# A recurrence and attention kernel on one core: the 16x16 inverse blocks are turned by VectorE on chip, K's products go to GpSimd, and the block products are spread over the steps

## The chip, the core and the metric

One core of a Trainium2 chip runs the whole program once. The metric is the device time of one execution in microseconds (us); lower is better. The engines are named as in the profile: PE is TensorE's matmuls, PEld its weight loads, DVE is VectorE, ACT is ScalarE, POOL is GpSimd, SP is the queue of SyncE that issues nearly all DMAs.

## What is computed

A recurrence over 768 tokens for 32 heads with a 40x40 state, then a causal attention with four experts, of which two are mixed for each token. The change touches the recurrence alone:

```python
for t in range(S):
    y[:, :, t] = np.einsum('bhd,bhde->bhe', rt, state)
    Sa = np.einsum('bhde,bhe->bhd', state, at)
    state_decay = state * wt[:, :, None, :] - np.einsum('bhd,bhe->bhde', Sa, bt)
    state = state_decay + np.einsum('bhd,bhe->bhde', vt, kt)
```

Then `_moe_ref` takes y as x: q, k, v of each expert, causal softmax, `a @ v @ wo`, mixed by the gate of the two chosen experts.

## The kernel before

**Stages.** The recurrence is done in chunks of 32 tokens. Six windows of four chunks make the 768 tokens, and in a window each chunk is done in four units of eight heads, so that there are 96 units, 16 to a window. Attention follows, from about 480 us on; it is not touched.

**A round.** The main loop of `recurrence` runs n = 0 to 99. In each round it issues one stage of several units, in the order of `MAIN`: u, g, y, f, t, k, v (the slots 0 to 6). Nothing is scheduled by the compiler here: every engine takes its instructions in the order in which the loop writes them. Extra work is hung on a round and a slot by tables of strings: `SIDE` and `SIDE2` (preparing the next window), `EARLY` (window 0) and `INV` (the inverse). In a string the parts between slashes are the slots, a digit is the group of heads, a letter is the step. n0 is 16(W-1) for window W; the numbers in the tables are rounds after n0, and window 1's `INV` is three rounds later.

**Preparing a window** (`prep`), for each of four groups i: a and s are scans over the decays (lines 247, 253); b and c fetch and invert four elements; x and y multiply a by the decays (line 256); k and l on VectorE (line 261), or p on GpSimd (line 258), multiply K and b by the decays into the tile KB, which m, n, N and M use as weights of the matmuls at line 274. VectorE moves their result with a mask into GL (line 277). o stores 32x32 blocks to a buffer in DRAM, Ld. w, v and e load the inputs of the next group (EW, EA and EK of one buffer each, so that each load waits for the last reader of its buffer). `START` does window 0 and 1 with p on GpSimd; windows 2 to 5 use k and l.

**The inverse** (`invert`). Each 32x32 block, one a partition, 128 at a time in the tile MT, is unit triangular. L loads MT from Ld; C sets the diagonal to one and zeroes the block M12; T runs the 28 instructions that invert both 16x16 diagonal blocks (line 305), by VectorE in window 0, by GpSimd in windows 1 to 5. Then MT must be turned, so that the block's columns lie on partitions (tile TT), and the first diagonal block must be there in a second form for the block products. In window 0 VectorE does this by five 32x32 transposes (lines 313 and 315, the second form into rows 32 to 63 of GL). In windows 1 to 5 it goes through DRAM: S stores MT to Td; X copies the 16x16 block on GpSimd (line 309) and stores it to Tx; eight rounds after L, I loads Tx into GL (line 320) and B loads TT from Td by four DMAs with rows of 32 elements (line 318).

**The block products** fill the off-diagonal 16x16 block of the inverse, for a chunk c of a window: F(c) is 32 matmuls of 16x32 by 16x16 (line 325) and an ACT copy into N (line 327), H(c) is 32 matmuls with N (line 333) and an ACT copy into TT (line 334). u and g of the chunk's units read TT and GL.

**SP** issues in order, and a DMA that waits for a buffer holds all behind it. The loads of a chunk (RB, VT, VG, RT) go out one chunk ahead.

Of the kernel before, what the change touches and what calls it, by code (L numbers as in the profile page):

```python
# [7 lines left out]
F32 = mybir.dt.float32  # L8
AF = mybir.ActivationFunctionType
# [8 lines left out]
NW, NG, C = 6, 4, 32  # L18
# [1 line left out]

START = """Z0 E4 0apbc E5 0sx 1a 1b 0y 1c 0d 1sx 2a 0n E7 0q E6 1py 0m 2b 0o 1d 2pcs 1n R1 1q 2x 3a 2Yq 1m 3b 2m 3p
2d 3csx 1o 3y 2n 4a 3m 2o 4pb 3n 4c 5a 3d 4sy 3o 5b L 3q R0 4x R2 V00 V10 5cs V11 5xp 6a C 5y V01 Z1 4q 6b
T28 B F0 4m H0 6cspx 4dno 6Y 7a E8 7b 5d 7c 5q 7spYx k0"""
EARLY = {
    0: "/7d/F1/7q 5n/5m 5o",
    1: "6n/H1/6m/6o",
# [20 lines left out]
    -5: "///3y 2N 3k 3l///3ve",
    -4: "///0M 3m 0dqo",
    -3: "///1M 3N 1dqo",
    -2: "///2Mdqo",  # L50
# [2 lines left out]

SIDE2 = {
    -15: "///0abcs///0w",
    -14: "/0kly//0X///0ev",
    -13: "///1abc",
    -12: "///1s 0m 1x///1w",
    -11: "///1y 1k 1l///1ve",
    -10: "///2a 1m 2bc",  # L60
    -9: "///2s 2x///2w",
    -8: "///2y 0N 2k 2l///2ve",
    -7: "///3a 2m 3bc",
    -6: "///3s 1N 3x///3w",
    -5: "///3y 2N 3k 3l///3ve",
    -4: "///0M 3m 0dqo",
    -3: "///1M 3N 1dqo",
    -2: "///2Mdqo",
    -1: "///3Mdqo",
}  # L70
INV = {0: "L", 1: "C T4", 2: "T6", 3: "T6", 4: "T6", 5: "T6", 6: "S X", 8: "I B", 12: "//F0", 13: "//F1 H0", 14: "//F2 H1", 15: "//F3 H2", 16: "//H3"}
YE = "AA"


# [32 lines left out]

def constants():
    f = np.float32
    cm = np.zeros((128, 211), f)  # L110
    cm[:, :128] = np.eye(128)
    j = np.arange(32)
    m = (j[:, None] < j[None, :]).astype(f)
    cm[:32, 128:160] = m
    cm[32:64, 128:160] = m
    cm[:32, 160:192] = m
    cm[32:64, 160:192] = -m
    cm[64:128, 128:192] = cm[0:64, 128:192]
    p = np.arange(128)
    cm[:, 195:211] = (p[:, None] % 32 - 16 == np.arange(16)[None, :])  # L120
    return {"CM": cm}


def recurrence(tc, ctx, I, xT, CM, early, tail=None):
    nc = tc.nc
    ep = early.enter_context(tc.tile_pool(name="early", bufs=1, side="right"))
    sp = ctx.enter_context(tc.tile_pool(name="rec", bufs=1))
    dp = ctx.enter_context(tc.tile_pool(name="scr", bufs=1, space=DRAM))
    pp = ctx.enter_context(tc.tile_pool(name="rps", bufs=4, space=PSUM))
    V, A, T, PL = nc.vector, nc.scalar, nc.tensor, nc.gpsimd  # L130
# [7 lines left out]
    def ring(name, shape, n):  # L138
        return [sp.tile(shape, F32, name=f"{name}{i}") for i in range(n)]
# [14 lines left out]
    GF = [ep.tile([128, 4104], F32, name="GLe")] + ring("GL", [128, 4104], 1)  # L154
    GL = [t[:, 0:4096].rearrange("p (g n s t) -> p g n s t", g=4, n=16, s=2) for t in GF]
    RB1 = ring("N", [128, 8, 32], 2)
    X1 = ring("X1", [128, 16, 16], 1)[0]
    MT = ring("MT", [128, 32, 32], 1)[0]
    TP = sp.tile([128, 112], F32, name="TP")
    TF = ring("TT", [128, 1032], 2)  # L160
    TT = [t[:, 0:1024].rearrange("p (n t) -> p n t", n=32) for t in TF]
# [4 lines left out]
    RB = ring("RB", [128, 16, 64], 2)  # L166
    XT = ring("XT", [104, 8, 128], 2)
    GT = ring("GT", [128, 8, 40], 4)
    Ld = [dp.tile([128, 32, 32], F32, name=f"Ld{i}") for i in range(2)]
    Td = [dp.tile([128, 32, 32], F32, name=f"Td{i}") for i in range(2)]  # L170
    Tx = [dp.tile([16, 128, 16], F32, name=f"Tx{i}") for i in range(2)]


    flat = lambda t: t.rearrange("p a b -> p (a b)")
    r20, r21 = R2
# [111 lines left out]

    def invert(w):

        M, gl, tt = MT, GL[w % 2], TT[w % 2].rearrange("q (p c s) t -> q p c s t", p=4, c=4)  # L290
        e = PL if w else V
        def ld():
            nc.sync.dma_start(M, Ld[w % 2])
        def cp():
            PL.memset(M.rearrange("p t j -> p (t j)")[:, ::33], 1.0)  # L295
            PL.memset(M[:, 0:16, 16:32], 0.0)
        def step(j):

            m, n = j, 15 - j
            tmp = TP[:, 0:2 * n * m].rearrange("p (b t i) -> p b t i", b=2, t=m)  # L300
            a = M[:, 0, 0:1]
            def two(t, c, *rest):
                return bass.AP(a.tensor, a.offset + 32 * t + c, [a.ap[0], [528, 2]] + [list(x) for x in rest])
            o, row, col = two(0, j + 1, (32, m), (1, n)), two(j, j + 1, (0, m), (1, n)), two(0, j, (32, m), (0, n))
            return [lambda: e.tensor_tensor(tmp, row, col, op=OP.mult), lambda: e.tensor_tensor(o, o, tmp, op=OP.add)]
        def st():
            nc.sync.dma_start(Td[w % 2], M)
        def turn():
            PL.tensor_copy(X1, M[:, 0:16, 0:16].rearrange("p t j -> p j t"))
            nc.sync.dma_start(Tx[w % 2].rearrange("k n r -> n k r"), X1)  # L310
        def bk():
            if w == 0:
                V.transpose(TT[0].rearrange("t n j -> t j n"), M.rearrange("n t j -> n j t"))
                for g in range(4):
                    V.transpose(gl[32:64, g].rearrange("k n s r -> k r (n s)")[:, 0:16], M[32 * g:32 * g + 32, 0:16])
                return
            for g in range(4):
                nc.sync.dma_start(TT[w % 2][32 * g:32 * g + 32], Td[w % 2][32 * g:32 * g + 32].rearrange("n t j -> t n j"))
        def ldx():
            nc.sync.dma_start(gl[32:48].rearrange("k g n s r -> k (g n s) r")[:, :, 0:16], Tx[w % 2])  # L320
        def first(c):
            p = ps([128, 8, 16])
            for x in range(8):
                for g in range(4):
                    T.matmul(p[32 * g:32 * g + 32, x], gl[32:48, g, x // 2 * 4 + c, x % 2], gl[32:48, g, x // 2 * 4 + c, x % 2, 0:16],
                             start=True, stop=True, tile_position=(32, 32 * g))
            A.activation(RB1[c % 2][:, :, 0:16], p, AF.Copy)
        def second(c):
            p = ps([128, 4, 2, 16])
            for x in range(8):  # L330
                for g in range(4):
                    q = slice(32 * g, 32 * g + 32)
                    T.matmul(p[q, x // 2, x % 2], RB1[c % 2][q, x], tt[q, x // 2, c, x % 2, 16:32], start=True, stop=True, tile_position=(32 * g, 32 * g))
            A.activation(tt[:, :, c, :, 16:32], p, AF.Copy)
# [114 lines left out]
    P = [prep(i) for i in range(24)]  # L449
# [471 lines left out]
def body(tc, I, out):  # L921
    with ExitStack() as ctx:
# [49 lines left out]
```

## Time and profile before

| | us |
|---|---|
| median of three runs | 737.15 (730.37 to 741.52) |
| the profiled execution | 736.43 |
| its span, from the first to the last instruction | 734.5 |
| mean granted share of the TensorE clock over the span | 0.857 |
| PE, DVE, ACT, POOL busy | 622.7, 508.0, 478.0, 210.7 |

The time of the profiled execution holds 1.9 us outside the span. The granted clock has two levels, 0.5 (1.2 GHz) and 1.0 (2.4 GHz); a share between them is a mean over a stretch. A busy PE is modelled from the pipeline, and a PE that is busy at 0.5 does half the work. In a timeline row the first number is the start in us from the span's start, the second the length, and in brackets stands how long the engine had been idle before and what ended that ("issue": nothing that the profile shows).

### The profile page before, as it was taken

How to read it: one execution, taken by the hardware profiler on the slowest of the kernel's cores; microseconds unless marked ns; L12 is line 12 of the kernel's file. 1: busy time of each engine (PE TensorE's matmuls, PEld its weight loads, DVE VectorE, ACT ScalarE, POOL GpSimd, SP SyncE). 2: the span in 40 equal slices, each digit the busy share in tenths (PEclk: the TensorE clock that was granted, in tenths of full speed). 3: DMA queues.
4: the chain of work that ended last, by engine and by line, in shares of the span. 5: the costliest groups of instructions: out<-in, count | busy, mean ns of one | idle time of the engine just before them, and what ended most of it. 6: DMA issues, size and time to landing. Idle time of an engine off the chain costs nothing. (4 is left out here: it accounts for less than half of the span.)

```text
span 734.5 us, 28507 instructions
## 1 busy us (share of the span) xinstructions
PE 622.7 (85%) x11921; PEld 539.0 (73%) x11921; DVE 508.0 (69%) x1226; ACT 478.0 (65%) x1304; POOL 210.7 (29%) x315
## 2 busy tenths in 40 slices
PE   4305889899899878998998899978989999999995
PEld 4204778798798767877887787877868877887773
DVE  8998889558558854894554258667797688658751
ACT  4592578569548754785587589845756666757762
POOL 5332152150006200620050001013565344433641
PEclk8555699669659986896699799998999999999998
DMA  7851368737627772674257178252113113211111
GB/s 202 201 130 39 74 161 164 186 105 158 163 56 188 149 160 57 172 164 114 65 168 113 47 218 229 65 156 75 45 52 97 50 42 85 58 32 44 37 37 42
DMA packets 105490, 80.80 MB, mean 110 GB/s; under 512 B 71304, under 2 KB 89480, under 8 KB 105352
## 3 DMA queue, kind: packets, MB, share of 16 engines
q1 hardware_dynamic: 105208, 78.77, 43.9%
q8 instruction: 97, 1.59, 0.9%
q14 instruction: 41, 0.34, 0.2%
q10 hardware_dynamic: 144, 0.11, 0.1%
HBM read 58.27 MB, written 14.29 MB: 99 GB/s over the span
## 5 line engine op out<-in xcount | busy, mean ns | idle before, releaser
L820 POOL TENSOR_TENSOR P<-P,m 128x128 f32<-128x128 f32 (+2 forms) x96 | 87.7, 936 | 95.3 <-DVE m L816 49.9
L401 DVE TENSOR_TENSOR R<-ps,CM 64x128 f32<-64x128 f32 x192 | 55.0, 286 | 70.6 <-PE ps L398 67.0
L408 PE MATMUL py<-R,LS 128*40 128x80 f32 x1536 | 92.4, 256 | 8.6 <-DVE R L401 4.8
L408 PEld LDWEIGHTS py<-R,LS 128*40 128x40 f32 x1536 | 71.0, 131 | 15.5 <-DVE R L401 6.4
L809 ACT ACTIVATE P<-sc,m 128x128 f32<-128x128 f32 (+2 forms) x96 | 60.8, 633 | 29.3 <-DVE m L808 24.8
L808 DVE TENSOR_REDUCE m<-sc 128x1 f32<-128x128 f32 (+2 forms) x96 | 59.3, 621 | 20.1 <-PE sc L801 18.8
L798 PE MATMUL sc<-ks,qs 128*128 128x384 f32 (+4 forms) x256 | 62.7, 346 | 5.4 <-ACT P L809 5.1
L274 PE MATMUL ps<-AB,KB 104*64 104x64 f32 x768 | 44.8, 273 | 26.3 <-DVE AB L256 15.6
L438 ACT ACTIVATE LS<-pt 40x320 f32<-40x320 f32 x92 | 39.6, 430 | 42.3 <-PE pt L434 39.1
L295 POOL MEMSET MT<- 128x32 f32 x6 | 0.9, 157 | 221.4 <-DMA MT<-Ld 221.4
L379 ACT ACTIVATE GT<-ps 32x160 f32<-32x160 f32 x192 | 56.4, 294 | 7.1 <-PE ps L377 3.2
L274 PEld LDWEIGHTS ps<-AB,KB 104*64 104x64 f32 x768 | 38.0, 181 | 29.8 <-issue 8.4
L387 ACT ACTIVATE R<-ps 32x160 f32<-32x160 f32 x192 | 56.5, 295 | 3.9 <-PE ps L385 0.4
L370 ACT ACTIVATE LS<-pt 64x320 f32<-64x320 f32 x96 | 41.5, 432 | 21.8 <-PE pt L366 20.4
L385 PE MATMUL ps<-GT,TT 128*33 128x40 f32 x1536 | 53.3, 221 | 0.3 <-ACT GT L379 0.2
L828 PE MATMUL pt<-CM,P 128*128 128x128 f32 x336 | 51.9, 275 | 1.9 <-ACT pt L834 1.7
L398 PE MATMUL ps<-RB,VU 128*64 128x64 f32 x768 | 49.4, 247 | 4.6 <-ACT VU L393 1.6
L434 PE MATMUL pt<-CM,R 104*104 104x104 f32 x368 | 50.2, 289 | 0.0
L798 PEld LDWEIGHTS sc<-ks,qs 128*128 128x128 f32 x256 | 40.7, 190 | 10.7 <-ACT P L809 9.5
L385 PEld LDWEIGHTS ps<-GT,TT 128*33 128x33 f32 x1536 | 40.6, 126 | 10.6 <-issue 3.4
L720 PE MATMUL pt<-xh,wq 128*128 128x384 f32 x192 | 43.0, 358 | 3.4 <-POOL xh L699 1.3
L398 PEld LDWEIGHTS ps<-RB,VU 128*64 128x64 f32 x768 | 37.4, 152 | 10.5 <-ACT VU L393 6.1
(161 smaller groups left out, 1466.9 us busy)
## 6 DMA issues: line engine op xcount, KB each, us to landing
RB<-in_RB SPq DMA_DIRECT2D x24, 320.0 KB
EK<-in_EK SPq DMA_DIRECT2D x18, 416.0 KB
ks<-ks SPq DMA_DIRECT2D x32, 192.0 KB
R<-in_VG SPq DMA_DIRECT2D x24, 208.0 KB
EW<-in_EA SPq DMA_DIRECT2D x18, 214.5 KB
R<-in_VT SPq DMA_DIRECT2D x48, 80.0 KB
R<-in_RT SPq DMA_DIRECT2D x24, 160.0 KB
xT<-XT SPq DMA_DIRECT2D x48, 80.0 KB
```

Of the source, the lines that this page charges most:

```text
L274: T.matmul(p_a[64 * x:64 * x + 64, y], kb[0:104, n, :], AB[0:104, n, :], start=True, stop=True, tile_position=(0, 64 * x))
L379: A.activation(gt[32 * g:32 * g + 32, s::2], p_g[64 * s:64 * s + 32], AF.Copy)
L385: T.matmul(p_u[64 * s:64 * s + 33, p], tt[:, o:o + 33], gt[:, h, :], start=True, stop=True, tile_position=(0, 64 * s))
L387: A.activation(hd(r2[32:64, 40 * h0:40 * h0 + 320], 40)[:, s::2], p_u[64 * s:64 * s + 32], AF.Copy, scale=-1.0)
L398: T.matmul(p_f[64 * x:64 * x + 64, y], vu[:, p, :], rb[:, 4 * g + p, :], start=True, stop=True, tile_position=(0, 64 * x))
L401: V.tensor_tensor(o[:, :, x], p_f[64 * x:64 * x + 64], mask[x][:, None, None, :].to_broadcast([64, 2, 2, 32]), op=OP.mult)
L408: T.matmul(py[64 * s:64 * s + 40, p], ls[:, h, :], m, start=True, stop=True, tile_position=(0, 64 * s))
L798: T.matmul(ps[:, c, 0:cw], QS[b][:, e, o], KS[b][:, e, z, k], start=(z == 0), stop=(z == 1 and not last), skip_group_check=True)
L808: V.tensor_reduce(m[:, 0, t:t + 1], ps[:, 0:ch, 0:cw], axis=AX.XY, op=OP.max, negate=True)
L809: later(DE, lambda: A.activation(pv, ps[:, 0:ch, 0:cw], AF.Exp, bias=m[:, 0, t:t + 1], accum_out=m[:, 1, t:t + 1]))
L820: PL.tensor_tensor(P[:, 0:n], P[:, 0:n], m[:, 3, t:t + 1].to_broadcast([128, n]), op=OP.mult)
L828: T.transpose(p[:, 128 * y:128 * y + 128], st["P"][t][:, 128 * c:128 * c + 128], ident)
```

## The change

The inverse of every window is turned on chip. After T, VectorE does B0 and B1 (the two halves of TT) and P (the first diagonal block into a new tile P), each one transpose of 128 partitions x 512 elements; S, X and I with their DMAs and the tiles Td, Tx and X1 are gone. Window 0 has the same three transposes in place of its five. C no longer zeroes M12: MT carries that block as loaded, so that TT holds it, turned, beside the inverse, and F takes TT's rows as weights in place of GL's. F's matmuls now sit at four row positions of the array (32g) in place of one, and the ACT copy behind F multiplies by a column of 0 and 1 in CM, which grows by one column. In `SIDE` and `SIDE2` each pair "k l" becomes "p", which puts 16 products of 104x1024 on GpSimd in place of 32 of 104x512 on VectorE. `INV` gives B0, P and B1 the rounds 8, 9 and 10, slot 3, and each F and each H a round of its own, 11 to 18, where five rounds, 12 to 16, held them before.

```diff
-T28 B F0 4m H0 6cspx 4dno 6Y 7a E8 7b 5d 7c 5q 7spYx k0"""
+T28 B0 B1 P F0 4m H0 6cspx 4dno 6Y 7a E8 7b 5d 7c 5q 7spYx k0"""
...
-    -14: "///0kl///0e",
+    -14: "///0p///0e",
...
-    -11: "///1y 1k 1l///1ve",
+    -11: "///1y 1p///1ve",
...
-INV = {0: "L", 1: "C T4", 2: "T6", 3: "T6", 4: "T6", 5: "T6", 6: "S X", 8: "I B", 12: "//F0", 13: "//F1 H0", 14: "//F2 H1", 15: "//F3 H2", 16: "//H3"}
+INV = {0: "L", 1: "C T4", 2: "T6", 3: "T6", 4: "T6", 5: "T6", 8: "///B0", 9: "///P", 10: "///B1", 11: "//F0", 12: "//F1", 13: "//H0", 14: "//F2", 15: "//H1",
+       16: "//F3", 17: "//H2", 18: "//H3"}
...
+    cm[:, 211] = p % 32 >= 16
...
-    X1 = ring("X1", [128, 16, 16], 1)[0]
+    P1 = ring("P", [128, 32, 16], 1)[0]
...
-            PL.memset(M[:, 0:16, 16:32], 0.0)
...
-        def st():
-            nc.sync.dma_start(Td[w % 2], M)
+        def bk(x):
+            q = slice(16 * x, 16 * x + 16)
+            V.transpose(TT[w % 2].rearrange("t n j -> t j n")[:, q], M.rearrange("n t j -> n j t")[:, q])
         def turn():
-            PL.tensor_copy(X1, M[:, 0:16, 0:16].rearrange("p t j -> p j t"))
-            nc.sync.dma_start(Tx[w % 2].rearrange("k n r -> n k r"), X1)
-        def bk():
-            if w == 0:
-                V.transpose(TT[0].rearrange("t n j -> t j n"), M.rearrange("n t j -> n j t"))
-                for g in range(4):
-                    V.transpose(gl[32:64, g].rearrange("k n s r -> k r (n s)")[:, 0:16], M[32 * g:32 * g + 32, 0:16])
-                return
-            for g in range(4):
-                nc.sync.dma_start(TT[w % 2][32 * g:32 * g + 32], Td[w % 2][32 * g:32 * g + 32].rearrange("n t j -> t n j"))
-        def ldx():
-            nc.sync.dma_start(gl[32:48].rearrange("k g n s r -> k (g n s) r")[:, :, 0:16], Tx[w % 2])
+            V.transpose(P1.rearrange("k n r -> k r n"), M[:, 0:16])
         def first(c):
             p = ps([128, 8, 16])
             for x in range(8):
                 for g in range(4):
-                    T.matmul(p[32 * g:32 * g + 32, x], gl[32:48, g, x // 2 * 4 + c, x % 2], gl[32:48, g, x // 2 * 4 + c, x % 2, 0:16],
-                             start=True, stop=True, tile_position=(32, 32 * g))
-            A.activation(RB1[c % 2][:, :, 0:16], p, AF.Copy)
+                    q = slice(32 * g, 32 * g + 16)
+                    T.matmul(p[32 * g:32 * g + 32, x], tt[q, x // 2, c, x % 2], P1[q, x // 2 * 8 + 2 * c + x % 2], start=True, stop=True,
+                             tile_position=(32 * g, 32 * g))
+            A.activation(RB1[c % 2][:, :, 0:16], p, AF.Copy, scale=CM[:, 211:212])
```

On PE, before, two rounds of window 4's block products (F at line 325, H at line 333, f at 398, K's and AB's matmuls at 274):

```order
L408 MATMUL py_78<-R_126,LS_122 40x80 x8
L325 MATMUL ps<-GLe 32x16 x32
L333 MATMUL ps<-TT_120,N_115 32x16 x32
L398 MATMUL ps<-RB_130,VU_129 64x64 x4
L274 MATMUL ps<-AB_110,KB_100 64x64 x4
...
L408 MATMUL py_79<-R_126,LS_122 40x80 x8
L325 MATMUL ps<-GLe 32x16 x32
L333 MATMUL ps<-TT_120,N_116 32x16 x32
L398 MATMUL ps<-RB_131,VU_128 64x64 x4
```

And the same two rounds now (F at line 314, H at line 322, f at 387):

```order
L397 MATMUL py_78<-R_126,LS_122 40x80 x8
L322 MATMUL ps<-TT_120,N_115 32x16 x32
L387 MATMUL ps<-RB_130,VU_129 64x64 x4
L273 MATMUL ps<-AB_110,KB_100 64x64 x4
...
L397 MATMUL py_79<-R_126,LS_122 40x80 x8
L314 MATMUL ps<-P_117,TT_120 32x16 x32
L387 MATMUL ps<-RB_131,VU_128 64x64 x4
```

A round holds one burst of 32 small matmuls where it held two.

On GpSimd, before, between the inverses of two windows stand only the copy for Tx and the two memsets:

```order
L305 TENSOR_TENSOR MT_118<-MT_118,TP 128x2x14
L309 COPY X_117<-MT_118 128x256
L295 MEMSET MT_118 128x32
L296 MEMSET MT_118 128x16x16
```

Now K's products (line 257, into KB) stand in the same queue: that of group 0 behind the tenth of the 28 inverse instructions (here of window 2), those of groups 1, 2 and 3 behind the last:

```order
L303 TENSOR_TENSOR MT_118<-MT_118,TP 128x2x10x5
L257 TENSOR_TENSOR KB_101<-EK_84,SUF_86 104x1024
L303 TENSOR_TENSOR TP<-MT_118 128x108
...
L303 TENSOR_TENSOR MT_118<-MT_118,TP 128x2x14
L257 TENSOR_TENSOR KB_102<-EK_84,SUF_86 104x1024
L257 TENSOR_TENSOR KB_103<-EK_84,SUF_86 104x1024
L257 TENSOR_TENSOR KB_104<-EK_84,SUF_86 104x1024
```

The product of group 1 is read by PE in the round after the one in which it is issued (1p in round n0'+5 of the window before, 1m in n0'+6).

On SP, before, at the turn of a window's inverse:

```order
L307 DMA Td_140<-MT_118 128x1024
L310 DMA Tx_142<-X_117 128x16x16
...
L320 DMA GLe<-Tx_142 16x128x16
L318 DMA TT_120<-Td_140 32x32x32 x4
L347 DMA R_127<-in_VT 32x640
L345 DMA R_125<-in_VG 32x1664
L189 DMA EA_83<-in_EA 104x512
```

Now these seven are gone, and the loads that stood behind them follow one another:

```order
L188 DMA EW_82<-in_EA 104x528
L336 DMA R_127<-in_VT 32x640
L334 DMA R_125<-in_VG 32x1664
L188 DMA EA_83<-in_EA 104x512
```

## Rows read from the trace of the kernel before

**Rows 1.** The page, part 2: granted TensorE clock in 40 slices of 18.4 us.

```profile
PEclk8555699669659986896699799998999999999998
```

**Rows 2.** Windows, line 422 (one a unit): stretch, us, busy (count), PEclk, DMA, GB/s.

```profile
130.52:162.12 31.60, 1.45 (x5) 0.62 0.59 145
178.71:223.44 44.73, 2.33 (x8) 0.66 0.55 115
246.68:302.87 56.19, 2.91 (x10) 0.73 0.54 116
329.28:364.98 35.70, 1.74 (x6) 0.67 0.41 91
397.38:426.88 29.50, 1.45 (x5) 0.77 0.27 70
```

**Rows 3.** The same view of line 422, two stretches between those.

```profile
223.44:246.68 23.24, 2.04 (x7) 1.00 0.78 196
367.33:397.38 30.05, 3.21 (x12) 1.00 0.70 141
```

**Rows 4.** Windows, all: stretch, us, PE, PEld, DVE, ACT, POOL busy, PEclk, DMA, GB/s.

```profile
223.44:246.68 23.24, 20.28 (x493) 17.62 (x491) 21.80 (x46) 20.35 (x61) 15.70 (x31) 1.00 0.78 196
367.33:397.38 30.05, 29.42 (x746) 26.32 (x744) 16.65 (x56) 27.09 (x79) 10.64 (x31) 1.00 0.70 141
```

**Rows 5.** Timeline, 320 to 338 us: SP, then who waits for its load.

```profile
325.38 4.17 SPq L318 DMA_DIRECT2D TT<-Td  x4
...
330.71 0.35 SPq L189 DMA_DIRECT2D EA<-in_EA  x1
...
336.15 0.68 DVE L256 TENSOR_TENSOR AB<-EA,SC 40x512 f32<-40x512 f32 x1 [4.15 <-DMA EA<-in_EA]
...
337.40 0.82 PE L408 MATMUL py<-R,LS 128*40 128x80 f32 x6 [1.63 <-DVE R L401]
```

**Rows 6.** Timeline, 405 to 409.5 us, PE; waits of PE; the page, part 3.

```profile
406.20 0.73 PE L325 MATMUL ps<-GL 16*32 16x16 f32 x64
...
406.82 0.72 PE L333 MATMUL ps<-TT,N 32*32 32x16 f32 x64
...
408.62 0.43 PE L398 MATMUL ps<-RB,VU 128*64 128x64 f32 x6 [0.82 <-issue]
...
PE ps L333 <- issue: 5.0, 5, 1.9
...
q8 instruction: 97, 1.59, 0.9%
```

**Rows 7.** Timeline, 55 to 65 us: the turn of window 0.

```profile
56.91 1.91 DVE L313 STREAM_TRANSPOSE TT<-MT 128x1024 f32<-128x1024 f32 x1
58.85 4.19 DVE L315 STREAM_TRANSPOSE GLe<-MT 32x512 f32<-32x512 f32 x4
...
63.09 1.03 PE L325 MATMUL ps<-GLe 16*32 16x16 f32 x58 [0.77 <-DVE GLe L315]
```

**Rows 8.** Groups by line and shape, DVE; timeline, 33 to 41 us.

```profile
L261 DVE TENSOR_TENSOR KB<-EK,SUF 104x512 f32<-104x512 f32 x32 | 22.5, 742 | 2.0 <-DMA EK<-in_EK 1.6
...
34.09 2.19 POOL L258 TENSOR_TENSOR KB<-KB,SUF 104x1024 f32<-104x1024 f32 x1 [6.11 <-DVE SUF L247]
34.93 1.37 DVE L249 COPY PC<-SUF 104x4 f32<-104x4 f32 x1
```

**Rows 9.** Timeline around 241 and 316 us: PE, DVE and POOL.

```profile
240.19 0.84 PE L274 MATMUL ps<-AB,KB 104*64 104x64 f32 x16 [1.14 <-DVE KB L261]
...
242.18 0.86 DVE L277 TENSOR_TENSOR GLe<-ps,CM 64x256 f32<-64x256 f32 x2
...
242.62 0.24 POOL L305 TENSOR_TENSOR MT<-MT,TP 128x28 f32<-128x28 f32 x1
...
315.99 0.69 PE L274 MATMUL ps<-AB,KB 104*64 104x64 f32 x16 [0.84 <-DVE KB L261]
316.00 0.64 POOL L309 COPY X<-MT 128x256 f32<-128x256 f32 x1
```

More of the change, by code (lines that the diff above doesn't have):

```diff
@@ L37 @@
     -15: "///0xy///0v",
-    -14: "///0kl///0e",
+    -14: "///0p///0e",
     -13: "///1abc",
     -12: "///1s 0m 1x///1w",
-    -11: "///1y 1k 1l///1ve",
+    -11: "///1y 1p///1ve",
     -10: "///2a 1m 2bc",
     -9: "///2s 2x///2w",
-    -8: "///2y 0N 2k 2l///2ve",
+    -8: "///2y 0N 2p///2ve",
     -7: "///3a 2m 3bc",
     -6: "///3s 1N 3x///3w",
-    -5: "///3y 2N 3k 3l///3ve",
+    -5: "///3y 2N 3p///3ve",
     -4: "///0M 3m 0dqo",
@@ L55 @@
     -15: "///0abcs///0w",
-    -14: "/0kly//0X///0ev",
+    -14: "/0py//0X///0ev",
     -13: "///1abc",
     -12: "///1s 0m 1x///1w",
-    -11: "///1y 1k 1l///1ve",
+    -11: "///1y 1p///1ve",
     -10: "///2a 1m 2bc",
     -9: "///2s 2x///2w",
-    -8: "///2y 0N 2k 2l///2ve",
+    -8: "///2y 0N 2p///2ve",
     -7: "///3a 2m 3bc",
     -6: "///3s 1N 3x///3w",
-    -5: "///3y 2N 3k 3l///3ve",
+    -5: "///3y 2N 3p///3ve",
     -4: "///0M 3m 0dqo",
@@ L109, in constants @@
     f = np.float32
-    cm = np.zeros((128, 211), f)
+    cm = np.zeros((128, 212), f)
     cm[:, :128] = np.eye(128)
@@ L169, in recurrence @@
     Ld = [dp.tile([128, 32, 32], F32, name=f"Ld{i}") for i in range(2)]
-    Td = [dp.tile([128, 32, 32], F32, name=f"Td{i}") for i in range(2)]
-    Tx = [dp.tile([16, 128, 16], F32, name=f"Tx{i}") for i in range(2)]
     flat = lambda t: t.rearrange("p a b -> p (a b)")
@@ L288, in invert @@
     def invert(w):
-        M, gl, tt = MT, GL[w % 2], TT[w % 2].rearrange("q (p c s) t -> q p c s t", p=4, c=4)
+        M, tt = MT, TT[w % 2].rearrange("q (p c s) t -> q p c s t", p=4, c=4)
         e = PL if w else V
@@ L338, in rows @@
                 t.pop(0)()
-        return dict(L=ld, C=cp, S=st, X=turn, B=bk, T=rows, I=ldx, F=first, H=second)
+        return dict(L=ld, C=cp, P=turn, B=bk, T=rows, F=first, H=second)
     def load_c(c, k):
@@ L926, in body @@
         FL = fp.tile([128, 20], F32, name="FL")
-        CM = fp.tile([128, 211], F32, name="CM")
+        CM = fp.tile([128, 212], F32, name="CM")
         FI = fp.tile([1, 1], I32, name="FI")
@@ L946, in body @@
                 moe(tc, c4, I, xT, out, CM[:, 0:128], pre[0])
-_INS = {"EA": (24, 104, 1040), "EK": (24, 104, 1024), "RB": (24, 80, 1024), "VT": (24, 32, 1280), "VG": (24, 32, 1664), "RT": (24, 40, 1024), "CM": (128, 211), "WD": (128, 7680),
+_INS = {"EA": (24, 104, 1040), "EK": (24, 104, 1024), "RB": (24, 80, 1024), "VT": (24, 32, 1280), "VG": (24, 32, 1664), "RT": (24, 40, 1024), "CM": (128, 212), "WD": (128, 7680),
         "WQK": (128, 1536), "WVG": (128, 780), "WO": (128, 640), "MM": (128, 256), "RAW": (32, 768, 6, 40)}
```

## Prediction

> **What bounds the kernel now.** I read the page's slices first: after the start the granted clock of PE swings between 0.5 and 1.0 until about 430 us, and is near 1.0 from there on [rows 1]. So I cut the recurrence into stretches where the clock stays at 1.00 and stretches where it does not, and counted in each the instruction of line 422, of which a unit has one. Five disturbed stretches, one a window, hold 5 + 8 + 10 + 6 + 5 = 34 rounds in 31.60 + 44.73 + 56.19 + 35.70 + 29.50 = 197.7 us, 5.82 us a round, at a clock of 0.62 to 0.77 [rows 2]. Between them a round takes 23.24 / 7 = 3.32 us, and 30.05 / 11 = 2.73 us in window 5, where nothing is prepared any more (the twelfth instruction there stands on the stretch's last instant) [rows 3]. In the calm stretches VectorE is the busiest, 21.80 of 23.24 us, ACT has 20.35; without preparation ACT has 27.09 of 30.05 and VectorE 16.65 [rows 4]. So the recurrence has two limits: VectorE where it is calm, and something that makes it stop and lose the clock once a window.
>
> The timeline shows two such things. First, SP spends 4.17 us from 325.38 on the four loads of TT, so that EA goes out at 330.71; VectorE stands 4.15 us for it, and PE behind it, and after that the clock is at its lower level, 1.2 GHz [rows 2, 5]. Second, in a product round F and H, 0.73 and 0.72 us, follow each other, and then PE stops for 0.82 us with nothing to wait for that the profile shows; line 333 alone has 5 such stops of 5.0 us [rows 6]. F and H are 64 weight loads and 64 matmuls each, 256 instructions together, and a packet of the instruction queue has 1.59 MB / 97 = 16.4 KB [rows 6], so I read these stops as PE's program arriving late. That is an inference, no row says it.
>
> The sum is made against the profiled execution, 736.4 us, which is 0.7 under the median.
>
> **Transposes of window 0.** 1.91 and 4.19 us stand between the inverse and F's start at 63.09 [rows 7]. Three transposes of 512 elements a partition are 1.91 / 2 = 0.95 to 4.19 / 4 = 1.05 each, 3.0 in all; PE waits there for nothing else. Gain 3.1 at most, none if VectorE then only waits for a load. I take -3.
>
> **The DMAs and the spreading.** With Td, Tx and TT's loads gone, EA is issued right behind the loads before it, and its 4 us wait should go; with one burst a round, PE has the rest of a round's instructions between two bursts. What is late next is the calm round's limit. I price the 34 rounds as calm ones: 29 x 3.32 + 5 x 2.73 = 109.9. To these come 40 bursts (8 a window, five windows). One takes PE 0.73 us [rows 6], while PE idles (23.24 - 20.28) / 7 = 0.42 a round in the calm [rows 4]; so a burst costs 0 to 0.73, and I take 0.4, near the difference: 16. That makes 126 for 198: -72. Both ends: -88 with bursts at nothing, and nothing at all if the clock falls all the same (the third rival).
>
> **Transposes of windows 1 to 5.** Three a window on VectorE, 1.0 us each. In window 5 VectorE has 13.4 us free in 11 rounds [rows 4], which hide them. In the four others VectorE is what bounds, and a row of B0, P and B1 stands in front of f, y's copies and the next scans: 12 x 1.0 = +12, between 0 and 15.7.
>
> **K's products.** VectorE loses 32 x 742 ns = 23.7 us [rows 8], 16 times 1.48 us. ACT is 0.41 us a round from being full [rows 4], and the products are 0.49 us a round (16 in the 48 rounds of preparation), so at most 20 of these are a gain. Against that, one product holds GpSimd 2.19 us, and a VectorE copy of four elements beside it took 1.37 us, until the product's end (34.93 + 1.37 = 34.09 + 2.19) [rows 8]. If each holds VectorE like this, 16 x 1.37 = 22 come back. Nothing in the trace of the recurrence is nearer to one end: I take 0, between -20 and +22.
>
> The Trainium skill, GPSIMD Engine Reference, section Engine selection, speaks against this part: a two-input elementwise operation is about twice as slow on GpSimd as on VectorE. Here it is 2.19 for 1.48, a factor of 1.5. By the page's factor a product would take 2.97 (an estimate), the waits of the next part would grow by some 1.6 us in each of four windows, and the sum would end near 707.
>
> **The queue on GpSimd.** A new wait. 1m needs the product of group 1, which now stands behind the 28 inverse instructions and the product of group 0. In the trace 1m's matmuls start at 240.19, waiting already for line 261, when the inverse ends at 242.86 [rows 9]. Two products of 2.19 behind that make 247.2. The pairs that VectorE loses bring PE to this place up to 3.0 us sooner; VectorE needs the result 2.0 us after PE's place (242.18). So up to 247.2 - 237.2 - 2.0 = 8 us are lost here; while VectorE stands, the inverse's steps are held up less, so I take 6. At 315.99 the inverse is just done [rows 9]: by the same working 5.4, I take 4. Beside the inverses of windows 1 and 2 no row can show it, since the rounds there ran slowly; I take 5 each, and 2 for the product of group 2, which in window 1's case is behind the inverse too. Sum +22, between 0 and 36. Behind 1m on PE stand t, k, v and the whole next round; behind its result on VectorE the decay; behind the product, SP holds EK's next load.
>
> **The clock after these waits.** A 4 us wait of VectorE preceded the fall in window 4 [rows 5], so four new waits of this length may each lower the clock for a round or two. A round at half the clock can at most double, +3.3; I take 1.5 each: +6, between 0 and 13.
>
> **Sum.** 736.4 - 3 - 72 + 12 + 0 + 22 + 6 = 701.
>
> **Rivals.** *GpSimd is in time.* If the rounds stay slow enough, or the inverse runs without VectorE's hindrance, 1m waits for nothing: 701 - 28 = 673. For it: the wait at 315.99 is the smaller one already. Against: at 240.19 PE was there 2.7 us before the inverse ended, with no product in the queue.
>
> *The loads are late anyway.* EA has one buffer and is loaded only when its last reader is done; if that, and not the DMAs in front, made it late, about half of the disturbed time stays: 701 + 36 = 737. For it: the DMA share is 0.78 in a calm stretch [rows 3], so the engines have little to spare. Against: SP issued EA 5.3 us after it began with TT [rows 5].
>
> *The products themselves keep the clock low (slower).* Small matmuls may be what the clock does not rise under: then eight rounds a window have them now, where five had, and each window in which the clock has fallen (after 1m's wait, say) runs its product rounds at the disturbed price: 8 x (5.82 - 3.72) = 16.8 us. All five: 701 + 84 = 785. From two windows on the gain of 35 is used up; two or three give 735 to 752. For it: the disturbed stretches reach past the wait that opened them, to the end of the product rounds [rows 2]. Against: window 0's F and H already stand one a round, and slice 5, in which they end, has 0.9 [rows 1].
>
> **How the numbers follow.** I give the forecast 0.54 (675 to 722), GpSimd in time 0.13, the late loads and the low clock in two or three windows together 0.19 (722 to 752), the low clock in nearly all 0.14. A change of under 2% can hardly be told from none here (the three runs before span 1.5%), so the bounds are 722 and 752: faster 0.67, same 0.19, slower 0.14. The likeliest case alone reaches from 675 to 722; for 8 in 10 the range goes down to 660, which takes in GpSimd being in time and part of the gain of K's products, and up to 750, which takes in a low clock in two windows.
>
> **What would show it.** Right: the wait of line 256 for EA gone; PE's "issue" stops at the products gone; a clock near 1.0 in the product rounds; rounds of 3.3 to 3.8 us there; F's start near 60 us; new waits of PE's line 273 for POOL's line 257, four or five of 2 to 6 us. Wrong: a clock of 0.5 through rounds 11 to 18 of a window; waits for EA as before; VectorE's two-input instructions beside line 257 at 2 us and more in most rounds, which would put K's products at the costly end.

## The result, and the profile after

The changed kernel takes 726.13 us (median of 15 runs) where the kernel before takes 736.54 (15 runs); the ratio is 0.9839, with a 95% interval of 0.9803 to 0.9876. The forecast was 701 in a range of 660 to 750. By the ratio, the kernel became faster by 12 us and not by 35. The ratio leaves out slow executions, one of them of 1268 us with the changed kernel. The profiled execution is 724.45 us, its span 722.7; against the span of before that is -11.8, and this is what the profile has to explain.

What was to go has gone. In window 0 the turn is three transposes, and F starts at 59.94 where it started at 63.09 [rows 7]. The timeline of the changed kernel:

```profile
56.94 1.97 DVE L306 STREAM_TRANSPOSE TT<-MT 128x512 f32<-128x512 f32 x2
58.80 0.99 DVE L308 STREAM_TRANSPOSE P<-MT 128x512 f32<-128x512 f32 x1
...
59.94 1.05 PE L314 MATMUL ps<-P,TT 16*32 16x16 f32 x64 [25.89 <-DVE P L308]
```

VectorE's wait for EA [rows 5] is not in the list of waits any more, and the page counts 63329 DMA packets where it counted 105490. But the number of instruction packets is the same, 97 [rows 6], and the granted clock [rows 1] is better without being whole:

```profile
PEclk9555698999899999989999989989999999999998
...
DMA packets 63329, 74.24 MB, mean 103 GB/s; under 512 B 29784, under 2 KB 47960, under 8 KB 63192
...
q8 instruction: 97, 1.59, 0.9%
```

To see where the 12 us are, I cut both kernels at the same rounds (a round ends where the decay of a unit starts, line 411, before at line 422). The product rounds are n0+9 to n0+18 of the five windows: 50 rounds with 38 of the 40 bursts (a burst is one F or H; the last two of window 1 run later) and seven of the 15 transposes of windows 1 to 5. The preparation rounds are n0+3 to n0+8 of the first four: 24 rounds with eight of K's 15 products after 85 us and six transposes. The columns of the view are the stretch, its length, the busy time of PE, PEld, VectorE, ACT and GpSimd with their instructions, then PE's granted clock, the DMA share and GB/s. Product rounds before:

```profile
114.73:162.12 47.39, 43.77 (x1247) 39.51 (x1246) 30.73 (x78) 29.64 (x90) 12.36 (x32) 0.75 0.68 152
183.51:232.82 49.31, 46.01 (x1240) 41.27 (x1240) 30.67 (x79) 28.75 (x87) 6.28 (x14) 0.69 0.54 130
256.33:309.08 52.75, 45.22 (x1255) 40.56 (x1253) 30.95 (x78) 29.75 (x90) 8.39 (x19) 0.74 0.54 125
329.28:376.37 47.09, 42.78 (x1215) 38.58 (x1216) 23.90 (x70) 27.96 (x85) 4.39 (x14) 0.75 0.47 111
392.12:436.77 44.65, 38.48 (x1205) 34.29 (x1198) 16.31 (x50) 27.68 (x83) 0.00 (x0) 0.85 0.51 118
```

The same rounds now:

```profile
116.08:158.71 42.63, 37.16 (x1149) 33.58 (x1146) 32.62 (x77) 31.01 (x92) 11.55 (x20) 0.91 0.53 138
186.18:229.74 43.56, 37.63 (x1234) 33.67 (x1234) 30.19 (x75) 28.84 (x86) 11.17 (x20) 0.88 0.52 132
254.62:299.59 44.97, 37.35 (x1241) 33.16 (x1240) 30.24 (x76) 29.02 (x87) 9.45 (x16) 0.92 0.47 119
327.57:368.11 40.54, 35.09 (x1197) 31.40 (x1198) 24.75 (x68) 27.07 (x81) 10.67 (x26) 0.92 0.40 100
384.81:425.61 40.80, 35.72 (x1178) 31.76 (x1176) 17.39 (x51) 27.41 (x81) 0.00 (x0) 0.92 0.49 144
```

That is 241.2 us before and 212.5 now, -28.7. The clock is at its lower level, 1.2 GHz, for a share of 2 x (1 - PEclk) of a stretch: by this 119 us of the product rounds before and 38 now. A round still takes 212.5 / 50 = 4.25 us; the calm round of [rows 3] takes 3.32. The preparation rounds, sums of the same view before and now:

```profile
sum 89.08, PE 79.53 PEld 69.49 DVE 77.87 ACT 74.64 POOL 30.68; mean PE 19.88 PEld 17.37 DVE 19.47 ACT 18.66 POOL 7.67
...
sum 106.99, PE 86.09 PEld 76.00 DVE 79.54 ACT 76.30 POOL 48.74; mean PE 21.52 PEld 19.00 DVE 19.88 ACT 19.07 POOL 12.18
```

That is +17.9. With -1.3 at the start (the decay of round 3 begins at 89.42, before at 90.75) and +1.0 in window 5's rounds n0+3 to n0+8, which neither sum holds, this makes -11.2 of the -11.8.

What stands in the way now is in the list of PE's waits (who waited for what: us in total, times, longest), from 85 to 480 us:

```profile
PE ps L273 <- POOL KB L257: 8.3, 4, 4.0
PE ps L366 <- issue: 6.6, 6, 1.9
PE ps L381 <- issue: 4.7, 4, 2.0
PE ps L322 <- issue: 4.5, 4, 3.0
...
PE py L397 <- issue: 2.9, 5, 1.3
PE ps L314 <- issue: 2.8, 4, 1.5
...
PE ps L387 <- issue: 2.0, 1, 2.0
PE pt L355 <- issue: 1.7, 1, 1.7
```

The first row is the forecast wait for GpSimd, four times with at most 4.0 us. The others are the stops for which the profile shows no cause. They were to go; with a last row of 0.6 they are 25.8 us in 26 stops. The same rows of before add up to 11.7 us in 12, the first of them in [rows 6] and

```profile
PE py L408 <- issue: 2.4, 3, 1.8
...
PE ps L325 <- issue: 2.2, 1, 2.2
```

The timeline shows two of the stops after the change, in rounds 44 and 45, and who waits for them:

```profile
268.07 0.73 PE L322 MATMUL ps<-TT,N 32*32 32x16 f32 x64
...
271.37 0.58 PE L355 MATMUL pt<-CM,KB 104*128 104x104 f32 x4 [1.72 <-issue]
...
273.36 0.73 PE L314 MATMUL ps<-P,TT 16*32 16x16 f32 x64
274.02 0.39 PE L387 MATMUL ps<-RB,VU 128*64 128x64 f32 x5
...
276.39 0.33 PE L387 MATMUL ps<-RB,VU 128*64 128x64 f32 x3 [1.99 <-issue]
...
276.76 0.59 DVE L390 TENSOR_TENSOR R<-ps,CM 64x128 f32<-64x128 f32 x2 [4.49 <-PE ps L387]
```

One burst in a round, and PE stops shortly behind it, once in the middle of eight equal matmuls of one product. The trace has the start of each packet of the instruction queue; beside five such stops it gives (us from the span's start):

```
packet starts   PE resumes   between
147.19          149.48       2.29
155.95          158.43       2.48
164.78          167.42       2.64
269.13          271.37       2.24
274.24          276.39       2.15
```

It is the same for all of them: the 26 stops end 2.2 to 2.8 us after the start of a packet of this queue, and the 12 of before 2.3 to 2.9, while the packets of the product rounds start about 4 us apart. The trace's record of the granted clock has 13 falls to the lower level between 85 and 480 us. Seven begin within 2.0 us behind the end of such a stop (of 1.4 to 3.0 us), three in or behind a wait for GpSimd (1.8 to 4.0), two behind other waits of PE (1.5 and 2.1); beside the last, at 192.10, PE has no wait over 1 us.

### The profile page after: what moved, and what is told of

It reads as the page before. It is cut to its first block, busy times and chain, and to the rows that moved or that the text cites. A ratio compares the mean times of both kernels' runs of the same rounds, so it can differ in the third digit from the quotient of the medians.

```text
span 722.7 us, 28465 instructions
## 1 busy us (share of the span) xinstructions
PE 595.0 (82%) x11921; PEld 514.5 (71%) x11921; DVE 512.5 (71%) x1207; ACT 479.8 (66%) x1304; POOL 237.3 (33%) x320
## 2 busy tenths in 40 slices
DMA packets 63329, 74.24 MB, mean 103 GB/s; under 512 B 29784, under 2 KB 47960, under 8 KB 63192
## 5 line engine op out<-in xcount | busy, mean ns | idle before, releaser
L397 PE MATMUL py<-R,LS 128*40 128x80 f32 x1536 | 85.7, 245 | 4.5 <-issue 2.9
L797 DVE TENSOR_REDUCE m<-sc 128x1 f32<-128x128 f32 (+2 forms) x96 | 59.4, 622 | 20.0 <-PE sc L790 18.7
L397 PEld LDWEIGHTS py<-R,LS 128*40 128x40 f32 x1536 | 65.9, 125 | 10.4 <-issue 3.9
L273 PE MATMUL ps<-AB,KB 104*64 104x64 f32 x768 | 41.1, 263 | 31.5 <-DVE AB L255 17.9
L257 POOL TENSOR_TENSOR KB<-EK,SUF 104x1024 f32<-104x1024 f32 x18 | 42.6, 2364 | 66.9 <-DMA EK<-in_EK 44.9
L273 PEld LDWEIGHTS ps<-AB,KB 104*64 104x64 f32 x768 | 35.3, 174 | 33.8 <-POOL KB L257 18.3
L387 PE MATMUL ps<-RB,VU 128*64 128x64 f32 x768 | 46.1, 238 | 8.7 <-DVE GLe L276 2.1
L374 PE MATMUL ps<-GT,TT 128*33 128x40 f32 x1536 | 51.2, 215 | 2.2 <-DVE GL L276 2.1
L423 PE MATMUL pt<-CM,R 104*104 104x104 f32 x368 | 47.2, 277 | 0.0
L374 PEld LDWEIGHTS ps<-GT,TT 128*33 128x33 f32 x1536 | 38.6, 120 | 11.8 <-DVE GL L276 2.2
L381 PE MATMUL ps<-CM,R 66*80 66x66 f32 x384 | 42.0, 234 | 5.1 <-issue 4.7
```

The lines of the kernel that those rows point to most:

```text
L273: T.matmul(p_a[64 * x:64 * x + 64, y], kb[0:104, n, :], AB[0:104, n, :], start=True, stop=True, tile_position=(0, 64 * x))
L374: T.matmul(p_u[64 * s:64 * s + 33, p], tt[:, o:o + 33], gt[:, h, :], start=True, stop=True, tile_position=(0, 64 * s))
L397: T.matmul(py[64 * s:64 * s + 40, p], ls[:, h, :], m, start=True, stop=True, tile_position=(0, 64 * s))
L797: V.tensor_reduce(m[:, 0, t:t + 1], ps[:, 0:ch, 0:cw], axis=AX.XY, op=OP.max, negate=True)
```

## The experiments

The theory after this reading: the calm base of the sum was right, and the bursts were mis-sized, because each brings 128 instructions that PE runs faster than its program arrives. The rival: VectorE's transposes, or the time that the bursts take PE, cost more than I had put. Beside it stands the question what GpSimd's queue costs. All ratios are to the kernel before on the same chip, with their 95% interval; a hundredth of it is 7.4 us, and a difference of two ratios is uncertain by about 5 to 9 us.

**K's products back on VectorE.**

```diff
-    -11: "///1y 1p///1ve",
+    -11: "///1y 1k 1l///1ve",
```

(and the other three rows of `SIDE` and `SIDE2` alike)

> The changed kernel with K's products back on VectorE, 32 of 742 ns. Theory 'GpSimd's queue': the rounds between a window's load of its triangle and its transposes (n0+3 to n0+8, windows 1 to 4) took 107.1 us after the change and 89.1 before, because block product 1m waits for line 257; without it they come back to 90 to 95, VectorE pays some of its 23.7 us in the product rounds, and the time is 708 to 718. Rival 'VectorE is the bound': what VectorE gets back costs more than the queue, 730 to 745.

Measured: 711.99 us, 0.9674 (0.9601 to 0.9748). The queue theory holds. The preparation rounds of this kernel, the sum of the windows view:

```profile
sum 94.86, PE 83.74 PEld 73.39 DVE 83.12 ACT 77.73 POOL 27.82; mean PE 20.93 PEld 18.35 DVE 20.78 ACT 19.43 POOL 6.96
```

They fall from 107.0 to 94.9, and the product rounds stay (213.7 for 212.5). So the third part of the change, K's products on GpSimd, costs 0.9839 - 0.9674 = 12 us, all of it in the preparation rounds, where eight of the 15 stand, those of groups 1 and 2. One stretch of product rounds of this run, that of window 3, has all eight whole bursts at the full clock:

```profile
244.50:285.98 41.48, 34.18 (x1205) 30.14 (x1205) 31.71 (x79) 28.91 (x86) 6.80 (x16) 1.00 0.50 130
```

So the small matmuls by themselves do not hold the clock down.

**The block products left out.**

```diff
-INV = {0: "L", 1: "C T4", 2: "T6", 3: "T6", 4: "T6", 5: "T6", 8: "///B0", 9: "///P", 10: "///B1", 11: "//F0", 12: "//F1", 13: "//H0", 14: "//F2", 15: "//H1",
-       16: "//F3", 17: "//H2", 18: "//H3"}
+INV = {0: "L", 1: "C T4", 2: "T6", 3: "T6", 4: "T6", 5: "T6", 8: "///B0", 9: "///P", 10: "///B1"}
```

> The changed kernel without the block products F and H of windows 1 to 5 (40 bursts of 64 matmuls and their ScalarE copies are left out, so the inverse of these windows stays without its lower left block). Theory 'program of PE': these bursts bring PE's program late, the stops that the profile calls issue (25.8 us in the recurrence) mostly go, the product rounds (n0+9 to n0+18, 4.33 us each) come near 3.6 and the time is 685 to 700. Rival 'transposes and the rest of VectorE': the bursts cost only the 0.4 us each that I had put, 708 to 716.

Measured: 688.67 us, 0.9374 (0.9315 to 0.9433). Product rounds, and the instruction queue on the page:

```profile
q8 instruction: 77, 1.26, 0.8%
...
sum 172.97, PE 151.64 PEld 135.05 DVE 136.63 ACT 134.61 POOL 35.58; mean PE 30.33 PEld 27.01 DVE 27.33 ACT 26.92 POOL 7.12
```

Two readings. Without the bursts the product rounds take 173.0 us, 3.46 a round, with the transposes in them: near my base of calm rounds. And 20 instruction packets are missing: 40 bursts x 128 = 5120 instructions, so a packet is 256 of them, and this queue does bring PE's program. The stops called issue are down to 2.0 us. The bursts, with their copies on ScalarE, cost 0.9839 - 0.9374 = 34 us, net of what came up in their place: PE's wait for GpSimd is 14.9 us in this run, where it was 8.3.

**Two bursts a round, as before.**

```diff
-       16: "//F3", 17: "//H2", 18: "//H3"}
+INV = {0: "L", 1: "C T4", 2: "T6", 3: "T6", 4: "T6", 5: "T6", 8: "///B0", 9: "///P", 10: "///B1", 12: "//F0", 13: "//F1 H0", 14: "//F2 H1", 15: "//F3 H2", 16: "//H3"}
```

> The changed kernel with F and H two in a round, in rounds 12 to 16 as before the change. Theory 'program of PE': two bursts in a row stop PE more, 732 to 742. Rival 'the spreading does nothing': 722 to 730, the same within noise.

Measured: 743.58 us, 1.0131 (1.0061 to 1.02), slightly past the upper forecast. With no way over DRAM left, the kernel is slower than before the change. Spreading is worth 1.0131 - 0.9839 = 21 us here, and is what the change's gain hangs on.

**The spreading alone, in the kernel before.**

```diff
-INV = {0: "L", 1: "C T4", 2: "T6", 3: "T6", 4: "T6", 5: "T6", 6: "S X", 8: "I B", 12: "//F0", 13: "//F1 H0", 14: "//F2 H1", 15: "//F3 H2", 16: "//H3"}
+INV = {0: "L", 1: "C T4", 2: "T6", 3: "T6", 4: "T6", 5: "T6", 6: "S X", 8: "I B", 11: "//F0", 12: "//F1", 13: "//H0", 14: "//F2", 15: "//H1",
+       16: "//F3", 17: "//H2", 18: "//H3"}
```

> The kernel before with F and H one in a round, rounds 11 to 18, and nothing else of the change. If the load of EA behind TT's loads is what lowers the clock, nothing is gained: 732 to 740. If the two bursts in a row did it, 715 to 725.

Measured: 725.42 us, 0.9881 (0.9823 to 0.9938). VectorE's waits here:

```profile
DVE AB L257 <- DMA EA<-in_EA: 10.9, 4, 4.1
...
sum 223.75, PE 191.90 PEld 170.16 DVE 132.59 ACT 141.90 POOL 33.54; mean PE 38.38 PEld 34.03 DVE 26.52 ACT 28.38 POOL 6.71
```

The waits for EA are all there, and yet the product rounds fall from 241.2 to 223.8 us, and the lower clock in them from 119 us to 61. So these waits were not what held the clock down through the product rounds; the pairs of bursts did more. The stops called issue are 28.7 us here, more than after the whole change.

**Few large matmuls in place of many small ones.**

```diff
+            if w:
+                for _ in range(6):
+                    T.matmul(p.rearrange("q x t -> q (x t)"), TF[w % 2][:, 0:128], TF[w % 2][:, 128:256], start=True, stop=True)
+                A.activation(RB1[c % 2][:, :, 0:16], p, AF.Copy, scale=CM[:, 211:212])
+                return
             for x in range(8):
                 for g in range(4):
```

(in F; in H alike, with N as weights. The loops below are left to window 0, so this kernel leaves out the block products; the copies stay, and H's goes to N)

> The changed kernel in which each burst of windows 1 to 5 is 6 matmuls of 128 by 128 in place of 64 small ones, about the same time of PE (8 of 104 by 104 took 0.92 us in line 423, so 6 take 0.7) with 12 instructions in place of 128; the block products are left out by this, and the copies stay. Theory 'program of PE': it is the number of instructions that costs, and the time falls near that without products, 690 to 702. Rival 'time of PE': a burst costs what it takes PE in a round that has no room, 718 to 730.

Measured: 720.38 us, 0.9731 (0.9673 to 0.9789), in the range of the rival. But my size was wrong, so this run does not test the two: the profile counts each such matmul as two, and a burst took PE 64.1 / 40 = 1.60 us, twice the 0.79 of the small ones. Even so the kernel is not slower, and the clock is 1.00 in all five stretches of product rounds. Twice the time of PE cost less than what the 104 instructions a burst (24 for 128) that were saved gave back. For the price, a run with half as many:

> As the run with few large matmuls, with three in place of six. The profile counts each of those six as two, and a burst took PE 64.1 / 40 = 1.60 us there, twice what I had put; a burst of 64 small ones takes (17.2 + 17.2) / 43.5 = 0.79 us in the changed kernel. So three are the same time of PE as the small ones, in 12 instructions in place of 128 (the block products are left out by this). Theory 'program of PE': 692 to 706, with the clock near 1.0 in the product rounds. Rival 'time of PE': 716 to 730.

Measured: 705.43 us, 0.9573 (0.95 to 0.9646). The groups of lines 313 and 326, and the sum of the product rounds:

```profile
L313 PE MATMUL ps<-TT 128*128 128x128 f32 x120 | 20.0, 307 | 0.4
L326 PE MATMUL ps<-TT,N 128*128 128x128 f32 x120 | 18.7, 292 | 0.0
...
sum 192.82, PE 179.75 PEld 158.39 DVE 136.09 ACT 143.87 POOL 37.51; mean PE 35.95 PEld 31.68 DVE 27.22 ACT 28.77 POOL 7.50
```

A burst takes PE (20.0 + 18.7) / 40 = 0.97 us, more than the small ones, and the kernel is 0.9839 - 0.9573 = 20 us faster. The product rounds are 19.7 us shorter; PE's idle time in them falls from 29.5 us (212.5 less its busy 183.0) to 13.1, its busy time by 3.2, so most of the gain is stops that are gone, and less of it a higher clock. Stops called issue are 2.6 us; the clock is 1.00 in three of the five stretches, 0.91 and 0.92 in the others. So I put 20 of the bursts' 34 us down to their number of instructions. The other 0.9573 - 0.9374 = 15 us are the time that they take PE, with their copies, which the run without products does not have. The matmuls differ from those of the change in shape as well as in number, and no run changes the number alone; that it is the number rests on the idle time that went and on where the stops end.

**The transposes twice.**

```diff
-INV = {0: "L", 1: "C T4", 2: "T6", 3: "T6", 4: "T6", 5: "T6", 8: "///B0", 9: "///P", 10: "///B1", 11: "//F0", 12: "//F1", 13: "//H0", 14: "//F2", 15: "//H1",
+INV = {0: "L", 1: "C T4", 2: "T6", 3: "T6", 4: "T6", 5: "T6", 8: "///B0 B0", 9: "///P P", 10: "///B1 B1", 11: "//F0", 12: "//F1", 13: "//H0", 14: "//F2", 15: "//H1",
```

> The changed kernel with each of the 15 transposes of windows 1 to 5 made twice. By my price, 12 of them on the path at 1.0 us, 736 to 740. If VectorE has become free in these rounds because PE is late, they cost nothing: 723 to 729.

Measured: 740.18 us, 1.0018 (0.9965 to 1.0072). 1.0018 - 0.9839 = 13 us for 15 transposes more, near the price that I had put. The product rounds of the profiled execution have the lower clock for 55 us in place of 38, so part of this can have come by the clock. The rival that the transposes cost more than I had put falls with this.

**Bursts cut in halves, in the same round and over more rounds** (K's products on VectorE). X is half of the eight x of F or H, and f, g and h, i are the halves:

```diff
-INV = {0: "L", 1: "C T4", 2: "T6", 3: "T6", 4: "T6", 5: "T6", 8: "///B0", 9: "///P", 10: "///B1", 11: "//F0", 12: "//F1", 13: "//H0", 14: "//F2", 15: "//H1",
-       16: "//F3", 17: "//H2", 18: "//H3"}
+INV = {0: "L", 1: "C T4", 2: "T6", 3: "T6", 4: "T6", 5: "T6", 8: "///B0", 9: "///P", 10: "///B1", 11: "//f0///g0", 12: "//f1///g1", 13: "//h0///i0", 14: "//f2///g2", 15: "//h1///i1",
+       16: "//f3///g3", 17: "//h2///i2", 18: "//h3///i3"}
...
-            for x in range(8):
+            for x in X:
```

> K's products on VectorE, and each burst cut into two of 32 matmuls, one at its place and one after k of the same round. As many instructions a round as with K's products on VectorE alone (712.0), but 64 in a row in place of 128. If the rate within a round matters: 698 to 708. If only the number in a round matters: 708 to 716.

Measured: 715.33 us, 0.9647 (0.9579 to 0.9716): the same as whole bursts (0.9674), with 40 copies on ScalarE more, which can hide a small gain.

```diff
+INVL = {**{k: v for k, v in INV.items() if k < 11}, 11: "//f0", 12: "//g0", 13: "//h0", 14: "//i0", 15: "//f1", 16: "//g1", 17: "//h1", 18: "//i1",
+        19: "//f2", 20: "//g2", 21: "//h2", 22: "//i2", 23: "//f3", 24: "//g3", 25: "//h3", 26: "//i3"}
```

> K's products on VectorE, and the halves of a burst one a round over rounds 11 to 26 (windows 2 to 5; window 1 has both halves in a round, as there is no time). Theory 'program of PE': with 64 instructions more a round in place of 128, in the rounds 19 to 26 too, where there is room, the stops go: 688 to 702. Rival: the next window's preparation fills PE's program in these rounds, and the stops only move, 708 to 720.

Measured: 698.93 us, 0.9447 (0.9387 to 0.9507), the fastest kernel of the study, 0.9839 - 0.9447 = 29 us faster than the change. Its product rounds:

```profile
110.47:150.41 39.94, 34.97 (x1073) 30.01 (x1072) 34.06 (x82) 30.11 (x94) 8.36 (x20) 0.96 0.55 142
178.71:215.08 36.37, 32.99 (x1001) 28.61 (x999) 31.63 (x80) 29.34 (x88) 5.78 (x14) 1.00 0.56 143
244.16:282.44 38.28, 33.98 (x1043) 29.66 (x1042) 31.50 (x79) 29.35 (x89) 8.12 (x18) 1.00 0.55 143
307.06:340.89 33.83, 31.21 (x961) 27.30 (x958) 24.78 (x70) 27.18 (x83) 4.95 (x16) 1.00 0.46 115
361.10:396.56 35.46, 32.29 (x976) 28.42 (x972) 17.42 (x52) 27.92 (x84) 0.00 (x0) 0.95 0.52 156
```

It counts how much of a burst a round holds, and not how that is cut within the round; half a burst is half the instructions and half of PE's time, and these two runs do not tell the two apart. The stops called issue are still 18.0 us in 24 stops (longest 2.3), as many us as with the halves in one round (17.4 in 21, longest 3.8). What differs in the profiled executions is the clock: it is at its lower level for 7 us of the product rounds here and for 72 there (in an execution 5 us over that run's median). Why the same sum of stops leaves the clock alone in one and not in the other is open.

**Window 1 spread as well** (its halves over rounds 14 to 27; its table is three rounds later, as ever).

```diff
+INV1 = {**{k: v for k, v in INV.items() if k < 11}, 11: "//f0///g0", 12: "//h0///i0", 13: "//f1", 14: "//g1", 15: "//h1", 16: "//i1",
+        17: "//f2", 18: "//g2", 19: "//h2", 20: "//i2", 21: "//f3", 22: "//g3", 23: "//h3", 24: "//i3"}
```

> The halves one a round over 16 rounds, K's products on VectorE, and window 1 too spread as far as its units allow (over rounds 14 to 27). Windows 2 to 5 gained 16 us by this; by its fifth window 2 to 4 us more: 693 to 699. If window 1 was not held by its bursts: 697 to 702.

Measured: 698.92 us, 0.9487 (0.9417 to 0.9558): no gain that can be told from the last.

**Half of K's products on GpSimd** (against the kernel with all of them on VectorE; bursts as in the change).

```diff
-    -8: "///2y 0N 2k 2l///2ve",
+    -8: "///2y 0N 2p///2ve",
...
-    -5: "///3y 2N 3k 3l///3ve",
+    -5: "///3y 2N 3p///3ve",
```

> Groups 0 and 1, which stand behind the inverse on GpSimd, have K's products on VectorE; groups 2 and 3 keep them on GpSimd. If only the queue behind the inverse costs, VectorE is relieved of 16 x 0.742 = 11.9 us in rounds 8 to 11, and the time is 702 to 710. If a product on GpSimd holds VectorE as long as it relieves it: 710 to 716.

Measured: 715.7 us, 0.9614 (0.951 to 0.9719), beside 0.9674 with all on VectorE. The interval holds both theories, so this run decides nothing.

**The long spreading with the way over DRAM** (the kernel before, with `INVL` for windows 2 to 5).

```diff
-        for r, line in INV.items():
+        for r, line in (INV if W == 1 else INVL).items():
```

> The kernel before, with the way over DRAM and K's products on VectorE as it had them, and with the halves of a burst one a round over rounds 11 to 26 (windows 2 to 5) or two a round (window 1). Theory: the way over DRAM costs by itself, the waits for EA (9.8 us) and what they do to the clock, so this stays 10 to 18 us above the same spreading with the turn on chip: 707 to 716. Rival: once PE's program is in time the rest has room for the loads, 696 to 704.

Measured: 711.92 us, 0.9648 (0.9559 to 0.9737), against 0.9447 with the turn on chip. The way over DRAM costs 15 us (12 against the 0.9487 of the run with window 1 spread as well, which ran on the same chip) also where the bursts are better spread. That is the turn as a whole, with all its DMAs, copies and transposes.

## Why the prediction was right in direction and wrong in size

Put together by the ratios, the three parts are: spreading -9 us (0.9881), the turn on chip -15 more (0.9674), K's products on GpSimd +12 (0.9839). The order matters: without the spreading, the other two together lose 10 (1.0131).

**The step that failed: "a burst costs 0 to 0.73, and I take 0.4".** The 38 bursts in the product rounds cost 212.5 - 173.0 = 39.5 us, 1.04 each, above my upper end; I had 15 for them. Over the whole kernel it is 34 / 40 = 0.85 each. The 0.4 fits what it counted, PE's time in a round with little room: the run with three large matmuls and the one without products differ by 15 us in 40 bursts, 0.37 each, though uncertain by 7 us and with the copies in it. What it left out is the arrival of the program, 20 us: mostly the stops themselves, and the clock, which fell behind seven of them. I had read these stops rightly from one row of before [rows 6], and then took it that one burst a round would end them: "with one burst a round, PE has the rest of a round's instructions between two bursts". The stops grew instead, from 11.7 to 25.8 us. They grew with the spreading: it alone, in the kernel before, with every wait for EA left, has 28.7. My reason would be that PE, at the higher clock, runs into the end of its program more often; that is argued, no run isolates it. The Trainium skill, Runtime: NRT & Kernel Launch, section Instruction fetch mechanics, says that an engine's program is refilled in blocks of 256 instructions, and that crossing a block is mostly hidden. The first agrees with the 20 packets that went with 5120 instructions; the second does not hold here, where bursts of 12 instructions and somewhat more time of PE are 20 us faster than those of 128.

**The base of calm rounds and the transposes were nearly right.** 40 rounds of windows 1 to 4 at 3.32 and 10 of window 5 at 2.73, with 6 us for the transposes of windows 1 to 4 that run in them (the other six run in the preparation rounds), make 166; without the bursts the 50 rounds took 173.0. Doubling the transposes cost 13 for my 12.

**The waits for EA were the wrong cause of the low clock, in part.** They opened the stretch of [rows 5], but with the bursts spread they stay (10.9 us) and the product rounds get 17.4 us shorter all the same. What they are worth lies within the 15 us of the turn, which also has other DMAs, a GpSimd copy and the transposes; no run takes the waits alone.

**The queue on GpSimd was right in mechanism and too dear.** I had 22 and 6 for the clock; with what VectorE was relieved of, it measures 12. One place shows it as forecast:

```profile
307.36 0.24 POOL L303 TENSOR_TENSOR MT<-MT,TP 128x28 f32<-128x28 f32 x1
307.55 2.17 POOL L257 TENSOR_TENSOR KB<-EK,SUF 104x1024 f32<-104x1024 f32 x1
309.75 1.26 DVE L246 TENSOR_TENSOR_SCAN SUF<-EW,D 104x528 f32<-104x528 f32 x1 [3.39 <-POOL KB L257]
309.77 1.12 PE L273 MATMUL ps<-AB,KB 104*64 104x64 f32 x16 [4.04 <-POOL KB L257]
```

The inverse of window 4 ends, the product of group 1 follows at once, and PE has stood 4.04 us for it. Beside the other inverses the wait was 2.0 us or less, where I had put 4 to 6. One wait I had not seen: VectorE's next scan overwrites SUF, which the product reads, and so it stands 3.39 us too (6.7 us in the recurrence). Of the +17.9 us in the preparation rounds, the run with K's products on VectorE leaves 5.8 unexplained. Six transposes run there now, which I had priced at 6. But the spreading alone, without a transpose, already takes these rounds from 89.1 to 96.4 us (the last two of window 1's bursts run in them by it), so how the 5.8 are made up stays open.

**What VectorE gained by losing K's products is not shown by itself.** I took 0. The product rounds, where seven of the 15 products stand, are 212.5 us with and 213.7 without them on GpSimd, which fits; in the preparation rounds it is mixed with the queue. A product takes 2.19 us there in the median, as in the start before [rows 8].

**The sum.** My terms with the rounds in which they lie: start -3; product rounds -62.3 (the -60, less 4.5 for the slow rounds 24, 39 and 40, 6 for six transposes and 0.8 for two bursts, which all count as preparation here: -60 + 4.5 - 6 - 0.8); preparation rounds +30.3 (+28 - 4.5 + 6 + 0.8): -35. Measured: -1.3, -28.7, +17.9, and +1.0 in window 5's preparation rounds: -11.2. Of the 34 us missed in the product rounds 24 are the bursts (39.5 - 15.2); the other 9 are there without them too. The 12 us by which the preparation rounds came out better than forecast made up for part of it: that is luck as to the sum, since the queue was priced too dear and the bursts too low.

**The rivals.** GpSimd was not in time; no wait for a load is left in the lists of PE and VectorE; and the low clock of the slower rival came in a milder form: 0.88 to 0.92 in the product rounds of every window, not 0.5 through them. Its mechanism, that small matmuls keep the clock low, does not fit window 3 of the run with K's products on VectorE (1.00 with all eight bursts). The time lies past my likeliest case (675 to 722), in the part to which I gave 0.19 for late loads or for a low clock in two or three windows; what put it there was neither, but bursts and stops in all five windows.

## What to carry to other kernels

Count the instructions that an engine runs in a stretch, not only their time: many tiny matmuls in a row can stop PE for its own program, and what shows it are its stops with the releaser "issue", the starts of the instruction queue's packets before their ends, and the number of these packets. Spread such bursts over as many rounds as their due times allow, and move nothing that PE needs soon into a queue behind a long job of a slow engine. Price a removed wait by a run, or a row, in which it stays and its suspected consequence goes; the wait that stands first in time need not be what makes the stretch slow.

## What the runs showed of the hardware that was not expected

Matmuls of 128 by 128 that took PE twice as long as the bursts they stood for (1.60 us for 0.79) made the kernel no slower, 0.9731 for 0.9839. And bursts cut in two within a round gained nothing (0.9647 for 0.9674), while the same halves in twice as many rounds gained 15 us (0.9447) and kept the clock between 0.95 and 1.00 in the product rounds, with hardly fewer us of stops. All stops without a cause, 26 after the change and 12 before, ended 2.2 to 2.9 us after a packet of the instruction queue had started.
